# Keys of two more units transposed by TensorE, and unit inputs loaded one iteration later

## The chip, the core and the metric

The kernel runs on one core of one Trainium2 chip, as one program. The metric is the device time of a run in microseconds (us). Five engines take part, each with its own in-order instruction stream: TensorE (PE, with its weight loads as PEld), VectorE (DVE), ScalarE (ACT), GpSimd (POOL) and SyncE (SP). SP issues nearly all DMA transfers; POOL issues those that scatter rows.

## What is computed

A linear attention over 4 batches, 8 heads, 768 positions and head size 48, and then a mixture of 8 experts, one chosen for each of the 3072 tokens:

```python
for t in range(S):                                   # attention, B=4, H=8, S=768, D=48
    kt, vt, rt = (k[:, :, t], v[:, :, t], r[:, :, t])
    cur = np.einsum('bhd,bhe->bhde', u[None] * kt, vt)
    y[:, :, t] = np.einsum('bhd,bhde->bhe', rt, state + cur)
    state = w[None, :, :, None] * state + np.einsum('bhd,bhe->bhde', kt, vt)

logits = x @ w_gate + modality_bias[modality_id]     # x: y as 3072 tokens x 384
e_idx = np.argmax(logits, axis=1)                    # gate_w: the softmax at e_idx
for e in range(8):
    mask = e_idx == e
    out[mask] = gate_w[mask, None] * (np.maximum(x[mask] @ w1[e], 0.0) @ w2[e])
```

## The kernel before

The attention is cut into 24 units, one for each batch and chunk of 128 positions; units 0 to 3 are chunk 0 of the four batches, and so on. The main loop (L1195) goes over iterations `i` = 0 to 22 and works on several units at once, each a stage apart. The order of the instructions of every engine is the order in which this loop writes them (a manual schedule), so an instruction that waits holds up everything behind it on its engine. SP too is such a queue.

Each unit has two inputs. `turned(i)` (L322) loads `ud`: receptances and keys, already transposed in memory, 96 partitions x 2 x 512 f32, into one of four buffers. For the units in `TURNED` (1 to 12) it loads the receptances alone, half as much. `lines(i)` (L331) loads `kv`: keys and values with one token on each partition, 128 x 2 x 384 f32, into one of five buffers. For a unit in `TURNED`, `keys_turned` (L341) has PE transpose the keys of `kv` into PSUM (`pkT`, four transposes), and `keys` (L379) multiplies that instead of the loaded half of `ud`.

In iteration `i` the stages that matter here are, in the order in which they are written: PE transposes the rows of unit i-2 (`raised`, `pxT`, units 7 to 11), then the keys of unit i+2 (`keys_turned`), and then computes the scores of unit i+1 (`scores`, `psc`, from `rc` and `kc`). DVE copies the bonus `d` of unit i. Once that `d` is there, SP issues `turned(i + 5)`: the call `pace` (L350) makes SP load one value of `d` so that the issue falls at this time. POOL computes `rc` of unit i+3 from `ud` (`decay`) and `kt` of unit i+2 from `kv` (`carry`); DVE computes `kc` of unit i+2 (`keys`) and then the factor `sx` of unit i-1 (`factor`). Once that is there, SP issues `lines(i + 4)`. Then come the mask products `at` of unit i+1 on DVE and the values `py` and the state of unit i on PE (`values`, `py`, `pst`, ending with the bonus of unit i+1 at L393).

From iteration 8 on the weights of the first expert are loaded too, in six pieces of 128 x 1024 f32 (`raw`, L905, 0.5 MB each). The expert's number is computed from the first four units at the end of iteration 8 (`order`), and SP reads it (`ctl`, L1128). Pieces 0, 1 and 2 follow at once, pieces 3, 4 and 5 at the ends of iterations 9, 10 and 11 (L1152 and the lines behind it). ScalarE takes norms of the pieces (L908), PE sums them (L923, in iterations 11 and 13), and ScalarE and DVE split the pieces into two f16 parts `whi` and `wlo` in iterations 11 to 13. From iteration 13 on PE runs pieces of the first expert's two products beside the units.

Of the kernel before, what the change touches and what calls it, by code (L numbers as in the profile page):

```python
# [44 lines left out]
DENSE = 6  # L45
FADED = range(4, 14)
SHARED = range(9, 14)
TURNED = range(1, 13)
RAISED = range(7, 12)

NE = 9
# [13 lines left out]
class _Kernel:  # L65
# [256 lines left out]
    def turned(self, i):  # L322
# [3 lines left out]
        ud = self.ud[i % len(self.ud)]  # L326
        m = n if i in TURNED else 2 * n
        self.nc.sync.dma_start(ud[LOW:TOP, :m], self.pd[b * NCH + c].rearrange("j d n -> (j d) n")[:, :m])
# [12 lines left out]
    def keys_turned(self, i):  # L341

        if i in TURNED:
            u = self.ctx_[i]
# [751 lines left out]
    def run(self):  # L1096
        nc, tc, m = self.nc, self.tc, self.m
        units = self.units = [(b, c) for c in range(NCH) for b in range(B)]
        NU = len(units)
# [35 lines left out]
        def chain(*gs):  # L1135
            for g in gs:
                yield from g
# [39 lines left out]
        def route(i, d, f, *args):  # L1177
            for lo, hi in GROUPS:
                if hi - 1 + d == i and lo in groups:
                    f(groups[lo], *args)  # L1180

        def each(i, *fs):
            for f in fs:
                if live(i):
                    f(i)


        def fill(n=1):
            while n and fills:
                g = fills.pop(0)  # L1190
                if next(g, fills) is not fills:
                    fills.append(g)
                    n -= 1

        for i in range(NU - 1):  # L1195
            if i == 0:
                each(i + 5, self.turned)
                each(i + 4, self.lines)
            each(i - 2, self.raised)
            each(i + 2, self.keys_turned)  # L1200
            each(i + 1, self.scores)
            if i + 1 > EARLY:
                each(i + 1, self.own_keys)
            route(i, 3, lambda u: fills.append(self.choose(u)))
            route(i, 5, lambda u: fills.append(chain(self.place(u), self.ahead(ahead[u["lo"]], u)) if u["lo"] in ahead else self.place(u)))
            up, down = ups.get(i), ups.get(i - 1)
            if up is not None:
                self.s_up(up, 0)
            if down is not None:
                self.s_high(down, 1)  # L1210
                self.s_down(down, 0)
            self.token(i - 1) if i else None
            if ups.get(i - 2) is not None:
                self.s_take(ups[i - 2])
            if i and i - 1 == self.grp["lo"]:
                groups[i - 1] = self.grp
            fill()
            each(i, self.taken) if i else None
            each(i - 1, self.settled_state)
            if i - 2 in RAISED:  # L1220
                self.flipped(i - 2)
            if 0 < i < NU - 5:
                self.pace(self.ctx_[i]["d"])
                each(i + 5, self.turned)
            for j in range(2):
                each(i - 1, lambda i: self.state(i, j))
                fill()
            if down is not None:
                self.s_low(down, 1)
                self.s_due(down)  # L1230
            begin.get(i, lambda: None)()
            late = i >= NU - 3
            for k in range(1 if late else 2):
                for d in (6, 7):
                    route(i, d, self.send, 1)
                if k == 0:
                    each(i + 3, self.decay)
            if ups.get(i - 2) is not None:
                self.s_give(ups[i - 2])
            each(i + 2, self.carry)  # L1240
            route(i, 4, self.sign)
            each(i + 2, self.keys)
            if i + 2 <= EARLY:
                self.own_turned(i + 2)
            if i:
                fac = self.factor(i - 1)
                for _ in fac:
                    fill()
                if i < NU - 4:
                    self.pace(self.ctx_[i - 1]["g"]["sx"][:, self.ctx_[i - 1]["at_g"] :])  # L1250
                    each(i + 4, self.lines)
            self.own(i, 0)
            each(i - 1, self.high)
            mid.get(i, lambda: None)()
            for j in range(2):
                each(i + 1, lambda i: self.causal(i, j))
                fill()
            self.own(i, 1)
            if late:
                for d in (6, 7):  # L1260
                    route(i, d, lambda u: (self.rest(self.ctx_[i]["dv"][:1, DM - 1 :]), self.send(u, 1)))
            each(i - 1, self.low)
            if up is not None:
                self.s_high(up, 0)
                self.s_low(up, 0)
            fill()
            each(i - 1, self.flip)
            fill()
            self.values(i)
            if up is not None:  # L1270
                self.s_up(up, 1)
            if down is not None:
                self.s_down(down, 1)
            for p in range(2):
                for h in range(2):
                    c, r = divmod(i + 1 - 2 * p - h, B)
                    if r == 0 and 0 < c < NCH - 1:
                        self.fade(c, slice(2 * p, 2 * p + 2), range(2 * h, 2 * h + 2))
            if any(hi - 1 + d == i for lo, hi in GROUPS for d in (4, 5)):
                fill(99)  # L1280
            route(i, 2, self.logits)
            route(i, 4, self.count)
            for f in at.get(i, ()):
                f()
            for k in turns.get(i, ()):
                self.s_turn(k)
# [4 lines left out]
        i, j = NU - 2, NU - 1  # L1291
# [207 lines left out]
```

## Time and profile before

| | us |
|---|---|
| median of three runs | 348.51 (348.34 to 350.56) |
| the profiled execution | 350.38 |
| its span, first to last instruction | 348.6 |
| PE busy in the span | 327.6 (94%) |
| VectorE busy | 216.7 (62%) |
| ScalarE busy | 179.4 (51%) |
| GpSimd busy | 157.1 (45%) |

The profile is one execution; times in it count from the first instruction of the span. A busy PE isn't PE at its peak: matmuls are pipelined and their ends are modelled. "Idle before" names how long an engine did nothing ahead of an instruction, and what ended that. "Issue" stands there when the profile shows nothing that the engine waited for. The granted clock is given as a share of full speed, where 1.00 is 2.4 GHz and 0.50 is 1.2 GHz. The main loop takes the first 165 us or so; after it come the remaining routing and the experts.

### The profile page before, as it was taken

What the parts mean: (1) busy time and instruction counts of PE and PEld (TensorE: products, weight loads), DVE (VectorE), ACT (ScalarE), POOL (GpSimd) and SP (SyncE); (2) the same over time, 40 slices, a digit from 0 to 9 for tenths busy, and PEclk for the clock granted to TensorE, in tenths of its full rate; (3) what the DMA queues carried; (4) which work ended last, traced back from release to release, by engine and by line L of the source; (5) the groups of instructions that cost most, each with busy time, mean ns of one, the idle gap of its engine ahead of it and who ended that gap; (6) DMA issues with size and microseconds to landing.
All of it is one profiled execution on the core that took longest, in us unless ns stands there. A gap on an engine that the chain in (4) does not pass through costs nothing. (4 is left out here: it accounts for less than half of the span.)

```text
span 348.6 us, 15394 instructions
## 1 busy us (share of the span) xinstructions
PE 327.6 (94%) x5555; PEld 268.1 (77%) x5555; DVE 216.7 (62%) x740; ACT 179.4 (51%) x476; POOL 157.1 (45%) x230
## 2 busy tenths in 40 slices
PE   7998999697999999999998999999999999999993
PEld 3787998596878888887886777776888887777771
DVE  8878889489897977684668633349333332233951
ACT  7776885956965658465531222256222224552921
POOL 8987788756746865342167411113111210121221
PEclk9999999969999999999999999999999999999998
DMA  6766798997569999693235531127731121112120
GB/s 198 218 161 162 153 183 279 307 254 155 140 127 222 230 242 267 110 183 87 71 115 171 189 100 45 45 53 219 210 67 46 45 54 37 45 45 68 23 58 4
DMA packets 56797, 46.95 MB, mean 135 GB/s; under 512 B 42920, under 2 KB 50359, under 8 KB 56496
## 3 DMA queue, kind: packets, MB, share of 16 engines
q1 hardware_dynamic: 53552, 36.86, 44.7%
q0 software_dynamic: 3200, 9.47, 8.2%
q8 instruction: 31, 0.51, 0.7%
q14 instruction: 14, 0.11, 0.1%
HBM read 26.03 MB, written 11.83 MB: 109 GB/s over the span
## 5 line engine op out<-in xcount | busy, mean ns | idle before, releaser
L998 PEld LDWEIGHTS <-whi 128*128 128x128 f16 x1248 | 72.4, 98 | 4.0 <-issue 1.0
L1007 DVE SCALAR_TENSOR_TENSOR hl<-phb,hh 128x256 f16<-128x256 f32 (+1 forms) x48 | 24.5, 511 | 68.6 <-ACTq L1430 38.9
L1061 PEld LDWEIGHTS <-hh 128*128 128x128 f16 x416 | 39.1, 98 | 29.6 <-ACT hh L1002 1.7
L998 PE MATMUL phb<-mxT,whi 128*128 128x128 f16 x768 | 51.0, 219 | 0.0
L410 ACT ACTIVATE dv<-kv,d 128x48 f32<-128x48 f32 x172 | 43.1, 324 | 3.4 <-issue 2.2
L1002 ACT ACTIVATE hh<-phb 128x256 f16<-128x256 f32 (+1 forms) x48 | 21.4, 454 | 41.1 <-PE phb L998 18.7
L998 PEld LDWEIGHTS <-wlo 128*128 128x128 f16 x624 | 37.7, 98 | 1.0 <-DVE wlo L944 1.0
L371 POOL TENSOR_TENSOR rk<-rc,kc 112x512 f32<-112x512 f32 x20 | 25.8, 1288 | 27.0 <-DVE ebx L309 10.7
L430 DVE TENSOR_TENSOR at<-psc,mask 128x512 f32<-128x512 f32 x48 | 31.6, 681 | 3.6 <-PE psc L424 3.6
L967 POOL TENSOR_TENSOR seenb<-otb,putb 128x1 int32<-128x1 int32 x16 | 4.5, 283 | 64.2 <-ACTq L1430 50.9
L424 PE MATMUL psc<-rc,kc 64*64 64x128 f32 (+1 forms) x768 | 28.8, 280 | 4.7 <-issue 3.1
L359 POOL TENSOR_TENSOR rc<-ud,powr 112x512 f32<-112x512 f32 (+1 forms) x25 | 30.8, 1237 | 3.6 <-PE pst L393 2.2
L1061 PEld LDWEIGHTS <-hl 128*128 128x128 f16 x208 | 19.4, 98 | 15.1 <-issue 2.5
L424 PEld LDWEIGHTS psc<-rc,kc 64*64 64x64 f32 (+1 forms) x768 | 21.8, 134 | 10.7 <-issue 5.4
L666 POOL DMA_INDIRECT rows<-row,posi x24 | 25.0, 1041 | 11.2 <-DVE pr L743 3.8
L1061 PE MATMUL po<-whi,hh 128*128 128x384 f16 x136 | 27.7, 326 | 2.2 <-ACT whi L939 1.2
L998 PE MATMUL phb<-mxT,wlo 128*128 128x128 f16 x384 | 29.3, 219 | 0.0
L1061 PE MATMUL po<-whi,hl 128*128 128x384 f16 x136 | 28.0, 326 | 1.2 <-PEq L1495 0.7
L1061 PE MATMUL po<-wlo,hh 128*128 128x384 f16 x136 | 27.7, 326 | 0.0
L461 PE MATMUL py<-kv,at 128*64 128x48 f32 x768 | 27.2, 225 | 0.0
L998 PE MATMUL phs<-mxT,whi 128*128 128x128 f16 x432 | 27.2, 219 | 0.0
L944 DVE SCALAR_TENSOR_TENSOR wlo<-raw,ws,whi 128x1024 f16<-128x1024 f32 (+1 forms) x20 | 25.9, 1322 | 1.9 <-ACT whi L939 1.2
(272 smaller groups left out, 621.0 us busy)
## 6 DMA issues: line engine op xcount, KB each, us to landing
kv<-in_pt SPq DMA_DIRECT2D x21, 384.0 KB
raw<-in_w SPq DMA_DIRECT2D x12, 512.0 KB
ud<-in_pd SPq DMA_DIRECT2D x12, 384.0 KB
raw<-in_w SPq DMA_DIRECT2D x2, 1536.0 KB, 6.8
ud<-in_pd SPq DMA_DIRECT2D x12, 192.0 KB
rows<-pad SPq DMA_DIRECT2D x10, 193.0 KB
kv<-in_pt SPq DMA_DIRECT2D x6, 192.0 KB
rows<-row,posi POOLq DMA_INDIRECT x24, 5.9
```

What stands on the lines that cost most here:

```text
L359: nc.gpsimd.tensor_mul(u["rc"][:TOP, s], u["rT"][:TOP, s], self.powr[:TOP, s])
L371: nc.gpsimd.tensor_mul(u["rk"][:TOP], u["rc"][:TOP], u["kc"][:TOP])
L410: nc.scalar.activation(u["dv"][:, sl], u["v"][:, sl], AF.Copy, scale=u["d"][:, h : h + 1])
L424: nc.tensor.matmul(u["ps"][j][s, pr * P : (pr + 1) * P], u["kc"][r, pr, s], u["rc"][r, pr, :], start=True, stop=True)
L430: nc.vector.tensor_mul(u["at"][:, j * NPR : (j + 1) * NPR, :], u["ps"][j].rearrange("p (q t) -> p q t", q=NPR), self.mask.unsqueeze(1).to_ ...
L461: nc.tensor.matmul(py[t, sl], u["at"][:, j * NPR + pr, t], u["v"][:, sl], start=c == h == 0, stop=h == H - 1, skip_group_check=True)
L666: i = nc.gpsimd.indirect_dma_start(out=self.rows, out_offset=bass.IndirectOffsetOnAxis(ap=u["posi"][:, b : b + 1], axis=0), in_=u["row"][: ...
L944: self.nc.vector.scalar_tensor_tensor(self.wlo[:, sl], self.raw[:, sl], sc, self.whi[:, sl], ALU.mult, ALU.subtract)
L998: self.nc.tensor.matmul(ph[:, q * P : (q + 1) * P], w[:, c0 : c0 + P], self.xT[:, xq, t * P : (t + 1) * P], start=i == q == 0, stop=i == l ...
L1002: self.nc.scalar.activation(self.hh[:, f0 : f0 + fb, t * P : (t + 1) * P], p3, AF.Relu)
L1007: self.nc.vector.scalar_tensor_tensor(self.hl[:, f0 : f0 + fb, r], p3, 0.0, self.hh[:, f0 : f0 + fb, r], ALU.max, ALU.subtract)
L1061: self.nc.tensor.matmul(po[:, :DM], h[:, f, t * P : (t + 1) * P], w[:, c0 : c0 + DM], start=first, stop=last)
```

## The change

`TURNED` grows by units 13 and 14: PE transposes their keys as well, four transposes each, and their `ud` loads shrink to half. In iteration 8 no unit input is loaded. From iteration 9 on `turned` is called for unit i+4 in place of i+5 and `lines` for unit i+3 in place of i+4, so that each load from unit 13's `ud` and unit 12's `kv` on is issued one iteration later than before, and the last ones in iterations 19 and 20.

```diff
--- before.py
+++ after.py
@@ -45,7 +45,8 @@
 DENSE = 6
 FADED = range(4, 14)
 SHARED = range(9, 14)
-TURNED = range(1, 13)
+HELD = 8
+TURNED = range(1, 15)
 RAISED = range(7, 12)
 
 NE = 9
@@ -1219,9 +1220,10 @@
             each(i - 1, self.settled_state)
             if i - 2 in RAISED:
                 self.flipped(i - 2)
-            if 0 < i < NU - 5:
+            n = 5 - (i > HELD)
+            if 0 < i < NU - n and i != HELD:
                 self.pace(self.ctx_[i]["d"])
-                each(i + 5, self.turned)
+                each(i + n, self.turned)
             for j in range(2):
                 each(i - 1, lambda i: self.state(i, j))
                 fill()
@@ -1246,9 +1248,9 @@
                 fac = self.factor(i - 1)
                 for _ in fac:
                     fill()
-                if i < NU - 4:
+                if i < NU - n + 1 and i != HELD:
                     self.pace(self.ctx_[i - 1]["g"]["sx"][:, self.ctx_[i - 1]["at_g"] :])
-                    each(i + 4, self.lines)
+                    each(i + n - 1, self.lines)
             self.own(i, 0)
             each(i - 1, self.high)
             mid.get(i, lambda: None)()
```

SP's queue around the end of iteration 8, before. `ud1` and `kv2` are the buffers of unit 13's `ud` and unit 12's `kv`; `ud2` is that of unit 14:

```order
L550 DMA_TRANSPOSE xT4_840<-row4_839 128x6x128
L328 DMA ud1_86<-in_pd 96x1024
L338 DMA kv2_91<-in_pt 128x2x384
L1128 TENSOR_LOAD ctl_370
L1128 ISA x2
L905 ISA
L905 DMA raw_275<-in_w12 128x1024
L905 ISA
L905 DMA raw_275<-in_w12 128x1024
L905 ISA
L905 DMA raw_275<-in_w12 128x1024
L328 DMA ud2_87<-in_pd 96x1024
```

The same place after the change (lines are one further down):

```order
L551 DMA_TRANSPOSE xT4_840<-row4_839 128x6x128
L1129 TENSOR_LOAD ctl_370
L1129 ISA x2
L906 ISA
L906 DMA raw_275<-in_w12 128x1024
L906 ISA
L906 DMA raw_275<-in_w12 128x1024
L906 ISA
L906 DMA raw_275<-in_w12 128x1024
L329 DMA ud1_86<-in_pd 96x512
L339 DMA kv2_91<-in_pt 128x2x384
L906 ISA
```

The two loads, which stood ahead of the read of `ctl` and so of the weights, now stand behind three pieces of weights, and the `ud` load is half as large.

PE at the start of iteration 12, before: the rows of unit 10 are transposed (`pxT10`), and the scores of unit 13 follow:

```order
L543 LDWEIGHTS row8_1396
L543 MATMUL pxT10_1821<-id16_157,row8_1396 128x128
L424 MATMUL psc13_0_1828<-rc13_1578,kc13_1718 64x128
L424 MATMUL psc13_1_1829<-rc13_1578,kc13_1718 64x128
L424 MATMUL psc13_0_1828<-rc13_1578,kc13_1718 64x128
```

The same place after the change:

```order
L544 LDWEIGHTS row8_1388
L544 MATMUL pxT10_1818<-id16_157,row8_1388 128x128
L348 MATMUL pkT14_1825<-id32_148,kv4_93 112x128 x4
L425 MATMUL psc13_0_1830<-rc13_1570,kc13_1715 64x128
L425 MATMUL psc13_1_1831<-rc13_1570,kc13_1715 64x128
L425 MATMUL psc13_0_1830<-rc13_1570,kc13_1715 64x128
```

Four transposes of unit 14's keys from its `kv` buffer stand between them; in iteration 11 the same is so for unit 13. PE's transposes for unit 12 in iteration 10 are where they were. Nothing else moves on PE; on VectorE two `kc` products read `pkT` instead of `ud`.

## Rows read from the trace of the kernel before

**Rows 1.** The page: engines (part 1), and the clock in 40 slices (part 2).

```profile
PE 327.6 (94%) x5555; PEld 268.1 (77%) x5555; DVE 216.7 (62%) x740; ACT 179.4 (51%) x476; POOL 157.1 (45%) x230
...
PEclk9999999969999999999999999999999999999998
```

**Rows 2.** PE in order of time: start us, us, line, operation, [idle before, releaser].

```profile
59.77 0.34 PE L543 MATMUL pxT<-id,row 128*128 128x128 f16 x3 [0.31 <-DVE off L760]
59.95 0.60 PE L347 MATMUL pkT<-id,kv 128*112 128x128 f32 x4
60.48 0.87 PE L424 MATMUL psc<-rc,kc 64*64 64x128 f32 x20
63.01 0.65 PE L424 MATMUL psc<-rc,kc 64*64 64x128 f32 x12 [1.66 <-issue]
63.60 0.88 PE L454 MATMUL py<-st,rc 112*64 112x96 f32 x16
...
66.69 0.51 PE L543 MATMUL pxT<-id,row 128*128 128x128 f16 x6
67.12 0.66 PE L424 MATMUL psc<-rc,kc 64*64 64x128 f32 x14
69.20 1.53 PE L424 MATMUL psc<-rc,kc 48*64 48x128 f32 x18 [1.42 <-issue]
70.67 0.19 PE L923 MATMUL py<-wssq,onesb 128*128 128x3 bf16 x1
...
76.95 1.10 PE L424 MATMUL psc<-rc,kc 64*64 64x128 f32 x32
```

**Rows 3.** Stretches: busy us of PE, PEld, DVE, ACT, POOL; clock, DMA share, GB/s.

```profile
55.50:58.00 2.50, 2.50 (x85) 2.50 (x81) 2.50 (x13) 2.32 (x7) 2.10 (x3) 1.00 0.77 178
58.00:60.00 2.00, 1.69 (x47) 1.46 (x45) 1.56 (x6) 1.07 (x4) 1.81 (x3) 1.00 0.97 346
60.00:64.50 4.50, 2.84 (x63) 2.25 (x62) 2.76 (x14) 4.44 (x13) 4.30 (x5) 1.00 1.01 308
...
69.00:76.00 7.00, 6.80 (x112) 6.45 (x113) 5.04 (x17) 3.14 (x7) 4.61 (x6) 0.51 0.92 271
...
84.00:88.00 4.00, 1.54 (x25) 1.16 (x24) 3.19 (x5) 0.91 (x5) 0.85 (x2) 1.00 0.25 53
...
98.00:156.00 58.00, 57.91 (x1223) 49.34 (x1221) 46.19 (x165) 38.65 (x124) 32.34 (x38) 1.00 0.93 201
...
98.50:101.00 2.50, 2.50 (x80) 2.42 (x77) 2.50 (x12) 2.24 (x9) 0.86 (x1) 1.00 0.59 157
240.00:244.00 4.00, 3.77 (x23) 1.92 (x22) 3.93 (x13) 1.29 (x3) 1.46 (x1) 1.00 1.03 363
63.00:69.15 6.15, 4.77 (x128) 4.23 (x127) 3.46 (x13) 6.08 (x18) 3.80 (x4) 1.00 1.05 315
```

**Rows 4.** The page, part 3: the queue named instruction: packets, MB, share.

```profile
q8 instruction: 31, 0.51, 0.7%
```

**Rows 5.** SP's queue in order of time: start us, us, what it issued.

```profile
51.05 0.38 SPq L338 DMA_DIRECT2D kv<-in_pt  x1
55.45 1.45 SPq L905 DMA_DIRECT2D raw<-in_w  x3
57.08 0.51 SPq L328 DMA_DIRECT2D ud<-in_pd  x1
57.77 0.51 SPq L338 DMA_DIRECT2D kv<-in_pt  x1
...
72.55 0.38 SPq L338 DMA_DIRECT2D kv<-in_pt  x1
...
98.26 0.34 SPq L328 DMA_DIRECT2D ud<-in_pd  x1
```

**Rows 6.** ScalarE in order of time: the first norm of the weights.

```profile
60.02 1.06 ACT L908 ACTIVATE junk<-raw 128x1024 f16<-128x1024 f32 x1 [0.95 <-DMA raw<-in_w]
```

**Rows 7.** GpSimd in order of time: the decayed receptances of unit 18.

```profile
101.37 1.28 POOL L359 TENSOR_TENSOR rc<-ud,powr 112x512 f32<-112x512 f32 x1
```

## The prediction

> **What bounds the kernel now.** I read the page first: TensorE (PE) is busy 94% of the span, and its clock row shows two slices below 9 in the body, the first of them slice 9, at 70 to 78 us [rows 1]. So I went to PE's timeline there, iterations 10 to 12 of the main loop. The reader is to see two idle times in the middle of a run of score matmuls (`psc`, L424): 1.66 us before 63.01 and 1.42 us before 69.20, both put to "issue", that is to nothing the profile shows [rows 2]. Only the first matmuls of such a run carry waits, so it isn't data. Then I read stretches: DMA is full from 58 us on (share 0.97 and more), and from 69 to 76 us the granted clock is 0.51, the 1.2 GHz level, though PE is busy; before and after it is 1.00, the 2.4 GHz level [rows 3]. Between the start of the work at 63 us and the second gap lie 128 matmuls and 127 weight loads [rows 3]; the queue named "instruction" moved 31 packets of 0.51 MB in all, 16.5 kB each [rows 4]. I read both gaps as PE waiting for its next block of instructions behind full DMA queues. That is an inference from spacing and load. From 98 to 156 us PE is busy 57.91 of 58 us [rows 3]: what is late before that is late at the end.
>
> The Trainium skill, page "Runtime: NRT & Kernel Launch", section "Instruction fetch mechanics", says that instructions come by DMA in blocks of 256, the next fetched while the present one runs, and calls the cost mostly hidden. The trace agrees with the 256 and not with "hidden": 1.66 and 1.42 us.
>
> **The change, part by part.** Times of the sum are those of the profiled execution: 350.38 us, a span of 348.6 and 1.8 around it. The median of the three runs is 348.51, 1.9 below; I add the sum to the median.
>
> (a) *Unit 12's keys and values arrive later.* Before, its `kv` load was issued at 51.05, 8.9 us ahead of the transposes that read it (`pkT`, 59.95, start of iteration 10) [rows 2, 5]. After the change it is issued where unit 13's is now, at 57.77, and unit 13's `ud` where unit 14's is now, at 57.08 [rows 5]. Both stand behind the three `raw` loads of 55.45 in SP's queue, and the order shows nothing that lets them past. If the queue is worked off in order, the bytes up to and with `kv` of unit 12 are 3 x 524 + 197 + 393 = 2163 kB (from the shapes). The stretches give 178 GB/s x 2.5 us = 445 kB by 58 us and 346 x 2 = 692 more by 60, 1137 together; the other 1026 kB at 308 GB/s take 3.3 us: 63.3 [rows 3]. From last byte to release I take raw's own row: its first 524 kB are through at 58 + 79/346 = 58.2 by the same count, and ScalarE, which waited for them, starts at 60.02 [rows 6]: 1.8 us. So `kv` is there at 65.1. Bounds: at 363 GB/s from 58 us (the fastest stretch) and with no release time 62.7; at 271 GB/s from 60 us 65.6 [rows 3]. From the start of `pkT` to the 20th `psc` matmul PE took 61.35 - 59.95 = 1.40 us, so the place that was reached at 63.01 is reached at 65.1 + 1.4 = 66.5 [rows 2]: **+3.5 us** (bounds +1.1 and +4.0). I take the middle estimate since it uses the stretch itself. The first instruction gap lies inside this wait and no longer counts.
>
> On this the Trainium skill, page "DMA: Bandwidth & Descriptors", section "Queues, rings and completion order", says that each DMA engine takes one queue's descriptors in ring order, while completion need not follow that order. No run here yet shows it for `kv`. By ring order the sum is as above; if a later load could finish early, the first rival below holds.
>
> Behind `pkT` on PE everything of iteration 10 queues up; on VectorE the key product `kc`, the factor `sx` of unit 9 and the mask product wait behind it. The `sx` also paces SP's next `kv` issue, so the loads of units 13 on slip as well; those DMA queues are then empty, which is (b).
>
> (b) *The second gap goes.* Its block of instructions would now be fetched during and after the wait, with 3.8 MB in place of 4.2 MB queued up to the fifth `raw` load, and part of that issued later. I take **-1.4 us** (bounds -1.4 and 0).
>
> (c) *Eight transposes more.* Four took 60.48 - 59.95 = 0.53 us of PE, start to start [rows 2]; two units: **+1.1 us** (bounds 0.5, if they fall into waits, and 1.1). VectorE's `kc` reads PSUM instead of SBUF for these two units, with the same shape; no cost. The two halved `ud` loads save 197 kB or 0.6 us of DMA at 346 GB/s for each, inside (a) and (b).
>
> (d) *Unit 14's keys are late too.* Its `kv` is issued in iteration 11, in the place of 72.55, which is 1.88 us after the small matmul L923 at 70.67 [rows 2, 5]; VectorE does L923's scales ahead of the pacing factor. A lone load of this size, issued at 98.26, had moved its 157 x 2.5 = 393 kB by 101.0, 2.7 us later [rows 3, 5]. So it is there 4.6 us after L923, or 6.4 with the release time of (a). PE arrives at `pkT` of unit 14 after 0.12 + 3.09 + 0.43 = 3.6 us at full clock (the values 63.60 to 66.69, then the turn of the rows until 67.12), or 6.3 at half clock [rows 2]. The wait is 1.0 to 2.8 us, or 0 to 0.1. I take **+1.6**, nearer the lower half of the first, as small matmuls of the count also stand there.
>
> (e) *The clock.* Before, it was low for 7 us after two gaps that sum to 3.1 us, which costs about 7 x 0.49 = 3.4 us [rows 3]. After, PE stands from 60.1 to 65.1, 5 us in one piece. I expect one such fall again, at another place: **0** (bounds -3.4, none, and +3.4, a second one at (d)).
>
> (f) *Loads with one iteration less of lead, iterations 12 to 20.* They cost nothing on PE: `rc` of unit 18 on GpSimd starts at 101.37, 3.1 us after the issue that would now be its own (98.26), so GpSimd may wait up to 1.4 us there [rows 5, 7]. Behind it on GpSimd queue `kt` and the row sends; `rc` is read by PE an iteration or more later. The cover is GpSimd's free time: 45% busy [rows 1]. If it were gone, each of some six iterations would give up to 1.4 us. Two late pairs of loads on SP (units 23 and 22) stand ahead of the transposing stores, which wait for the same factor anyway.
>
> Sum: 3.5 - 1.4 + 1.1 + 1.6 + 0 = **+4.8 us**, 348.5 + 4.8 = 353.3 us.
>
> **Rivals.** *Unit 12's load is hidden* (not slower). If later loads share the DMA engines with `raw`, `kv` could be there by 61.6, and then PE reaches 63.01 as before. That is the point from which it decides. For it: both gaps then shrink to at most the first, and the clock may stay up. Against it: the first 524 kB of `raw` themselves took until 60.02 [rows 6], and even issued alone at 57.77 with the 2.7 us of a lone load `kv` is there at 60.5 at the earliest. It would give -1.4 - 3.4 + 1.1 + 0.8 (half of (d)) = -2.9: 345.6 us.
>
> *The clock doesn't fall, or is back before PE has its data.* For it: at 84 to 88 us PE was busy only 1.54 of 4 us and the clock stayed at 1.00 [rows 3]. Against: two shorter gaps brought it down at 69 us. Sum 4.8 - 3.4 = +1.4: 349.9 us.
>
> *It falls twice*, the second time at unit 14's wait: 4.8 + 3.4 = +8.2: 356.7 us.
>
> *Absorbed.* The 2.5 us in which PE stands at 84 to 88 us could take up part of the delay [rows 3]. Against it: that wait is for VectorE and ScalarE, whose work there follows PE's scores of unit 13 and so slips with them. With 2.5 us taken up: +2.3, 350.8 us.
>
> **How the numbers follow.** Forecast 0.47 (its own range 350.5 to 356); hidden load 0.15; clock saved 0.15; second fall 0.13; absorbed 0.10. One per cent, 3.5 us, is about what a measurement of this kernel can tell from no change: below 345.0 is faster, above 352.0 slower. Slower: 0.36 of the forecast's 0.47, all of the second fall and a little of "absorbed", 0.51. Faster: a third of the hidden load, 0.05. The rest, 0.44, lies within 1%. The range from 346 to 357 leaves out half of the hidden load, half of the second fall and the forecast's tails, less than 0.2.
>
> **What would show it.** Right: in PE's timeline of the changed kernel `pkT` of unit 12 starts some 5 us after the transposes of unit 8's rows, released by a DMA of `kv`; no issue gap follows in `psc` of unit 12; `pkT` of unit 14 waits again for 1 to 3 us; the granted clock is low for about 7 us once; from iteration 14 on every start is 4 to 5 us later, to the end. Wrong: `pkT` of unit 12 starts before 61.6 (then (a) falls, and the queue isn't worked off in order); the gaps stay (then they aren't instruction blocks kept back by DMA); or the starts agree again from 98 us on (absorbed).

## The result, and the profile after

The changed kernel took 353.31 us (median of six runs, 351.86 to 355.69), the kernel before 349.22 beside it on the same chip: a ratio of 1.0124, with a 95% interval from 1.0086 to 1.0163. Measured again on another chip it was 353.72 against 349.65, 1.0115 (1.0064 to 1.0167). So the change costs about 4.1 us. The profiled execution of the changed kernel took 352.36 us, with a span of 350.6.

The page of the changed kernel, engines (part 1) and the clock in 40 slices (part 2):

```profile
PE 328.5 (94%) x5563; PEld 269.0 (77%) x5563; DVE 212.0 (60%) x740; ACT 179.2 (51%) x476; POOL 155.8 (44%) x230
...
PEclk9999998598999999999999999999999999999999
```

Beside [rows 1] there are eight matmuls more, and the slow slices are 7, 8 and 10 (8, 5 and 8 tenths; a slice is 8.8 us) in place of 9. PE's timeline shows why. Its columns are those of [rows 2]; lines are one further down than before.

```profile
53.00 1.10 PE L425 MATMUL psc<-rc,kc 64*64 64x128 f32 x32
...
58.60 0.34 PE L544 MATMUL pxT<-id,row 128*128 128x128 f16 x3 [0.31 <-DVE off L761]
64.55 1.10 PE L348 MATMUL pkT<-id,kv 128*112 128x128 f32 x4 [5.61 <-DMA kv<-in_pt]
65.58 1.99 PE L425 MATMUL psc<-rc,kc 64*64 64x128 f32 x32
71.63 0.51 PE L544 MATMUL pxT<-id,row 128*128 128x128 f16 x6
71.97 0.60 PE L348 MATMUL pkT<-id,kv 128*112 128x128 f32 x4
72.50 1.10 PE L425 MATMUL psc<-rc,kc 64*64 64x128 f32 x32
73.54 0.18 PE L924 MATMUL py<-wssq,onesb 128*128 128x3 bf16 x1
77.36 0.24 PE L621 MATMUL pr<-oh,warm 128*128 128x8 f16 x4 [0.56 <-DVE row L612]
77.64 0.49 PE L544 MATMUL pxT<-id,row 128*128 128x128 f16 x6
78.83 0.62 PE L348 MATMUL pkT<-id,kv 128*112 128x128 f32 x4 [0.70 <-DMA kv<-in_pt]
79.38 1.47 PE L425 MATMUL psc<-rc,kc 64*64 64x128 f32 x32
85.52 1.28 PE L425 MATMUL psc<-rc,kc 64*64 64x128 f32 x32
89.60 0.17 PE L924 MATMUL py<-wssq,onesb 128*128 128x3 bf16 x1 [0.69 <-ACT row L498]
95.49 1.10 PE L425 MATMUL psc<-rc,kc 64*64 64x128 f32 x32
```

The transposes of unit 12's keys (64.55) wait 5.61 us for their `kv`. The score matmuls of units 11 (65.58) and 12 (72.50) then run in one piece: both issue gaps of [rows 2] are gone. Unit 13's transposes (71.97) don't wait, unit 14's (78.83) wait 0.70 us.

To compare places one thing has to be taken out. The scores of unit 10, which the change doesn't touch, start at 53.00 here and at 54.13 in the kernel before; this execution was 1.13 us ahead by then. The same place in the kernel before, the scores of unit 15, and two waits that will matter, from its PE timeline:

```profile
54.13 1.10 PE L424 MATMUL psc<-rc,kc 64*64 64x128 f32 x32
...
85.49 0.68 PE L998 MATMUL phs<-mxT,wlo 128*128 128x128 f16 x9 [0.86 <-DVE wlo L944]
87.77 0.17 PE L923 MATMUL py<-wssq,onesb 128*128 128x3 bf16 x1 [1.60 <-ACT row L497]
...
93.65 1.10 PE L424 MATMUL psc<-rc,kc 64*64 64x128 f32 x32
```

With 1.13 us added to the times after the change, the scores of unit 11 start 6.2 us later than before (60.48 to 66.71), those of unit 12 6.5 (67.12 to 73.63), of unit 13 3.6 (76.95 to 80.51), and of unit 15 3.0 (93.65 to 96.62). The span's end is 3.1 later; the two profiled executions themselves are 2.0 us apart, so they show less than the 4.1 of the medians. What is lost at unit 12's keys is partly given back twice: once in iterations 11 and 12, where before had its second gap and its slow clock, and once between 84 and 90 us, where before waited 0.86 and 1.60 us and the changed kernel only 0.69.

The second profile of the changed kernel, from the other chip, needs no such shift: its scores of unit 10 start at 54.04. The scores of units 10 and 15 in its PE timeline:

```profile
54.04 1.10 PE L425 MATMUL psc<-rc,kc 64*64 64x128 f32 x32
...
96.51 1.10 PE L425 MATMUL psc<-rc,kc 64*64 64x128 f32 x32
```

There unit 12's transposes start at 66.23, 6.3 us later than before, the scores of unit 13 4.1 later (at 81.06) and those of unit 15 2.9 later. The clock falls only once, from 61.4 to 71.6 us.

Stretches of the changed kernel (columns as in [rows 3]): the two with the clock at 0.50, then the settled loop, then the whole disturbed part, 55 to 108 us:

```profile
59.30:69.40 10.10, 4.85 (x64) 4.18 (x66) 3.19 (x16) 6.47 (x16) 5.22 (x6) 0.51 0.79 258
80.00:83.40 3.40, 3.40 (x62) 3.07 (x54) 2.91 (x12) 3.36 (x10) 2.58 (x4) 0.50 0.77 187
...
98.00:156.00 58.00, 57.22 (x1175) 47.98 (x1172) 45.69 (x163) 36.88 (x121) 32.34 (x36) 1.00 0.95 210
55.00:108.00 53.00, 44.48 (x983) 39.25 (x980) 40.49 (x134) 37.81 (x98) 32.18 (x33) 0.87 0.68 186
```

and the last of these for the kernel before:

```profile
55.00:108.00 53.00, 46.32 (x1065) 40.99 (x1055) 44.10 (x140) 40.05 (x104) 35.48 (x37) 0.94 0.80 204
```

From such rows each kernel's loss can be added up: what PE stood still in these 53 us, and half of what it was busy at the lower clock. Before: 53 - 46.32 = 6.7 still, and 6.80 x 0.49 = 3.3 by the clock (the stretch 69 to 76 us in [rows 3]), 10.0 in all. After: 8.5 still, 4.85 x 0.49 + 3.40 x 0.50 = 4.1 by the clock, and 1.1 for the eight transposes, 13.7. The second profile of the changed kernel gives 13.6 (9.9 still, 5.37 x 0.49 = 2.6 by the clock, 1.1). The difference, 3.7 us, lies between the 3.0 by which unit 15 lags in the same two executions and the 4.1 of the medians, so the sum is good to some 0.7 us. It is used once more below.

SP's queue (SP's start us, us for the issue) and two waits of GpSimd, changed kernel:

```profile
54.29 3.20 SPq L906 DMA_DIRECT2D raw<-in_w  x3
57.62 0.35 SPq L329 DMA_DIRECT2D ud<-in_pd  x1
58.15 0.41 SPq L339 DMA_DIRECT2D kv<-in_pt  x1
...
75.42 0.38 SPq L339 DMA_DIRECT2D kv<-in_pt  x1
```

```profile
63.44 1.25 POOL L360 TENSOR_TENSOR rc<-ud,powr 112x512 f32<-112x512 f32 x1 [5.17 <-DMA ud<-in_pd]
...
136.64 1.71 POOL L360 TENSOR_TENSOR rc<-ud,powr 112x512 f32<-112x512 f32 x1 [2.86 <-DMA ud<-in_pd]
```

The reader sees unit 12's `kv` issued at 58.15, 3.9 us behind the first of three weight pieces (compare [rows 5]), and at hand 6.4 us later. Unit 13's `ud`, just ahead of it, keeps GpSimd waiting for 5.17 us.

### The profile page after: what moved, and what is told of

It is laid out like the page before. It is cut to its first block, busy times and chain, and to the rows that moved or that the text cites. A ratio compares the mean times of both kernels' runs of the same rounds, so it can differ in the third digit from the quotient of the medians.

```text
span 350.6 us, 15408 instructions
## 1 busy us (share of the span) xinstructions
PE 328.5 (94%) x5563; PEld 269.0 (77%) x5563; DVE 212.0 (60%) x740; ACT 179.2 (51%) x476; POOL 155.8 (44%) x230
## 5 line engine op out<-in xcount | busy, mean ns | idle before, releaser
L360 POOL TENSOR_TENSOR rc<-ud,powr 112x512 f32<-112x512 f32 (+1 forms) x25 | 31.6, 1266 | 13.8 <-DMA ud<-in_pd 13.1
L667 POOL DMA_INDIRECT rows<-row,posi x24 | 25.5, 1064 | 10.8 <-issue 3.7
L425 PE MATMUL psc<-rc,kc 48*64 48x128 f32 (+1 forms) x768 | 28.2, 285 | 0.8 <-POOL rc L360 0.8
L425 PEld LDWEIGHTS psc<-rc,kc 48*64 48x64 f32 (+1 forms) x768 | 21.8, 137 | 6.4 <-issue 2.2
L462 PEld LDWEIGHTS py<-kv,at 128*64 128x64 f32 x768 | 26.1, 143 | 0.7 <-issue 0.7
```

Source lines behind the costliest of these rows:

```text
L360: nc.gpsimd.tensor_mul(u["rc"][:TOP, s], u["rT"][:TOP, s], self.powr[:TOP, s])
L425: nc.tensor.matmul(u["ps"][j][s, pr * P : (pr + 1) * P], u["kc"][r, pr, s], u["rc"][r, pr, :], start=True, stop=True)
L462: nc.tensor.matmul(py[t, sl], u["at"][:, j * NPR + pr, t], u["v"][:, sl], start=c == h == 0, stop=h == H - 1, skip_group_check=True)
L667: i = nc.gpsimd.indirect_dma_start(out=self.rows, out_offset=bass.IndirectOffsetOnAxis(ap=u["posi"][:, b : b + 1], axis=0), in_=u["row"][: ...
```

## The experiments

All ratios are against the kernel before on the same chip. The chips differ in level (its medians were 344.97, 349.65, 344.85 and 347.06 us in the four groups), so only ratios are compared between groups.

### Unit 12's `kv` early, all else changed

```diff
-                if i < NU - n + 1 and i != HELD:
+                if i < NU - n + 1 and i != HELD + 1:
```

> The changed kernel, but unit 12's kv is loaded in iteration 8 again, ahead of the weights; everything else as changed. If the late kv of unit 12 makes the loss: the wait of 5.6 us in front of pkT of unit 12 is gone, and the time falls from 353.3 to 349 to 351 us (what stays is 1.1 us for the transposes and up to 1.6 for unit 14). If the eight transposes or the late ud loads make it: 352.5 to 354 us, with no wait at pkT of unit 12 and the lateness at another place.

1.0017 (0.9978 to 1.0056). Nearly all of the loss is gone. PE's timeline, the transposes of units 12, 13 and 14:

```profile
58.60 0.60 PE L348 MATMUL pkT<-id,kv 128*112 128x128 f32 x4
...
67.32 1.10 PE L348 MATMUL pkT<-id,kv 128*112 128x128 f32 x4 [2.83 <-DMA kv<-in_pt]
...
75.77 0.62 PE L348 MATMUL pkT<-id,kv 128*112 128x128 f32 x4 [0.33 <-DMA kv<-in_pt]
```

Unit 12's don't wait any more. What no theory foresaw: now unit 13's wait 2.83 us, since they came early enough to meet their own `kv`, which is still behind the weights. The loss of one late load, 1.0124 and 1.0115 less 1.0017, is 0.98 to 1.07%, some 3.6 us, with some 2 us either way by the intervals.

### The transposes alone

```diff
-TURNED = range(1, 13)
+TURNED = range(1, 15)
```

(in the kernel before)

> The kernel before, with the keys of units 13 and 14 transposed by TensorE and all loads issued where they were. If the late kv makes the loss: 349 to 350.5 us, that is at most the 1.1 us of the transposes more than before, or slightly less if 394 kB less of ud shorten the two idle times in psc. If the transposes make it: 352.5 to 354 us.

1.0038 (0.9991 to 1.0085): +1.3 us, with an interval from -0.3 to +2.9. PE's timeline, the transposes of units 12 and 13:

```profile
58.61 0.60 PE L347 MATMUL pkT<-id,kv 128*112 128x128 f32 x4
...
67.99 1.10 PE L347 MATMUL pkT<-id,kv 128*112 128x128 f32 x4 [4.04 <-DMA kv<-in_pt]
```

Again unit 13's keys wait, for a `kv` that was issued at 57.77, right behind the weights as in the kernel before [rows 5]. Turning the keys puts PE's transposes in front of that load. There is no issue gap in the scores of units 11 and 12 here. The wait can't be what replaces the first gap, since the scores of unit 11 run from 59.14, ahead of it; what differs there is told under the blocks of instructions below.

### The later loads alone

```diff
-TURNED = range(1, 15)
+TURNED = range(1, 13)
```

(in the changed kernel)

> The changed kernel's load order with the keys of units 13 and 14 loaded, not transposed. If the late kv of unit 12 makes the loss: pkT of unit 12 waits some 5 to 6 us as in the changed kernel; unit 14's wait and 1.1 us of transposes are gone; 351 to 352.5 us. If the transposes make it: 349.2 us, no change against before. If the late ud makes it: 353 us or more, since ud is twice as large for units 13 and 14.

1.0249 (1.0147 to 1.0352) from four runs: far more than the first two theories said. The third, late `ud`, allowed such a time, but the next section shows late `ud` loads alone to cost nothing. A second measurement:

> The changed kernel with the keys of units 13 and 14 not turned (their ud loads in full, no transposes for them), a second time. Its first figure, 1.0249 of the time before from four runs, lies 4.3 us above that of the changed kernel (1.0124), though it has 1.1 us less work on TensorE. Theory (the 197 kB more of unit 13's ud, which stand ahead of unit 12's kv, and the 197 kB of unit 14's cost far more than the 0.6 us each of the prediction): 1.020 to 1.030, and unit 12's kv again lands 12.5 us or more after the issue of the first weight piece. Rival (scatter of the landing, which was 12.2 us in another kernel with half the load ahead): 1.008 to 1.016, landing 10.3 to 11.5 us.

1.016 (1.0103 to 1.0218). Unit 12's transposes in PE's timeline, first run and second:

```profile
68.31 1.10 PE L348 MATMUL pkT<-id,kv 128*112 128x128 f32 x4 [8.69 <-DMA kv<-in_pt]
```

```profile
65.77 1.10 PE L348 MATMUL pkT<-id,kv 128*112 128x128 f32 x4 [5.73 <-DMA kv<-in_pt]
```

The first weight piece was issued at 54.97 and 55.39, so `kv` was at hand 13.3 and 10.4 us after it, by the same program. Most of the first figure may be scatter of that landing; that is not shown. The later loads alone account for the whole loss. Both figures lie above both of the changed kernel, though the intervals overlap, so whether turning the keys of units 13 and 14 costs its 1.1 us, or saves something by the halved `ud` ahead of `kv`, stays open.

### Late `ud`, `kv` as early as before

```diff
-                if i < NU - n + 1 and i != HELD:
+                if i < NU - 4:
                     self.pace(self.ctx_[i - 1]["g"]["sx"][:, self.ctx_[i - 1]["at_g"] :])
-                    each(i + n - 1, self.lines)
+                    each(i + 4, self.lines)
```

> The changed kernel, but all kv loads are issued in the iterations of before; only the ud loads come an iteration later, and units 13 and 14 are transposed. If the late kv makes the loss: GpSimd still waits about 5 us for unit 13's ud, which nobody on PE feels, and the time is 348 to 350.5 us. If the late ud makes it: 352.5 to 354 us.

1.0032 (0.9986 to 1.0078), no more than the transposes alone (1.0038). Late `ud` loads cost nothing that can be measured, though GpSimd waits for them. The first run of this section kept unit 12's `kv` alone early and comes out the same, so the later `kv` of units 13 on cost nothing that can be measured either.

### Two weight pieces moved behind unit 12's `kv`

```diff
-            plan(O + max(q - 2, 0), first(q))
+            plan(O + max(q - 2, 1 if q else 0), first(q))
```

> The changed kernel, with pieces 1 and 2 of the weights issued after unit 12's kv (in iteration 9) in place of ahead of it. If the queue is worked off in order, 1048 kB less stand ahead of kv: it lands some 3.4 us sooner after the first piece's issue, about 6 to 7 us after it instead of 10, pkT of unit 12 waits 1.5 to 3 us, and the ratio to before falls to 1.000 to 1.006. If all loads under way share the engines, so that the order within the queue does not matter: the landing, the wait of 5 to 6 us and the ratio of 1.012 stay.

1.0049 (1.0005 to 1.0094), beside 1.0115 for the changed kernel on the same chip:

> The changed kernel once more, beside the kernel before on this chip: a ratio of 1.009 to 1.016, that is some 3 to 5.5 us more, with a wait of 5 to 6 us for unit 12's kv. If the first measurement was a matter of the chip or of the clock's phase: a ratio of 1.00.

SP's queue and PE's wait with the two pieces behind, then PE's wait in the changed kernel run beside it:

```profile
54.58 0.38 SPq L906 DMA_DIRECT2D raw<-in_w  x1
55.41 0.33 SPq L329 DMA_DIRECT2D ud<-in_pd  x1
56.38 1.08 SPq L339 DMA_DIRECT2D kv<-in_pt  x1
57.68 1.43 SPq L906 DMA_DIRECT2D raw<-in_w  x3
```

```profile
62.57 1.10 PE L348 MATMUL pkT<-id,kv 128*112 128x128 f32 x4 [3.34 <-DMA kv<-in_pt]
```

```profile
66.23 1.10 PE L348 MATMUL pkT<-id,kv 128*112 128x128 f32 x4 [6.19 <-DMA kv<-in_pt]
```

With 1048 kB less ahead of it `kv` is at hand 8.0 us after the first piece's issue instead of 10.8 (10.3 in the first profile), and PE waits 3.34 us instead of 6.19. The ratio fell as the order of the queue has it, but the landing came 1 us later than the 6 to 7 us expected. The trace shows more. Each of these loads has sixteen completion updates, as many as there are DMA engines (read here as one for each engine's share), and PE starts within 0.06 us of the last. The eighth update comes 6.0 us after the first piece's issue here and 9.4 us after it in both profiles of the changed kernel: 3.4 us sooner, the figure that was expected for 1048 kB. The last one trails the eighth by 2.0 us here, by 0.9 and 1.4 there. So what stands ahead in SP's queue does hold `kv` back.

### Less behind unit 12's `kv`

```diff
-            plan(O + max(q - 2, 0), first(q))
+            plan(O + max(q - 2, 0) + (q == 3), first(q))
```

> The changed kernel with the fourth weight piece (0.5 MB), which is issued 0.6 us behind unit 12's kv, put off by one iteration; what stands ahead of kv is unchanged. Theory that the queue is worked off in order: kv of unit 12 lands as in the changed kernel, 10.0 to 10.8 us after the issue of the first piece, and the wait of unit 12's transposes stays 5 to 6.2 us. Rival (what is issued behind shares the DMA engines with kv): it lands 1 to 1.5 us sooner, 8.7 to 9.3 us after the first piece's issue, with a wait of 4 to 4.7 us.

One run, 350.9 us. PE's wait, and a stretch of that wait:

```profile
66.67 1.10 PE L348 MATMUL pkT<-id,kv 128*112 128x128 f32 x4 [7.58 <-DMA kv<-in_pt]
```

```profile
65.00:66.60 1.60, 0.00 (x0) 0.00 (x0) 0.00 (x0) 0.00 (x0) 1.44 (x2) 0.50 0.14 52
```

That is 12.2 us after the first piece's issue (54.44): neither theory's number. The completion updates show where the scatter lies. Unit 13's `kv` in the kernel with the transposes alone and in the one with late `ud` has the same 2163 kB up to and with it, so there are five loads to compare, and three with more or less:

| kernel, load | kB up to and with it | first update | eighth | last, us after the first piece's issue |
|---|---|---|---|---|
| changed, two profiles, unit 12 | 2163 | 8.8, 8.6 | 9.4, 9.4 | 10.2, 10.8 |
| less behind, unit 12 | 2163 | 9.5 | 10.2 | 12.2 |
| late `ud`, unit 13 | 2163 | 9.4 | 10.2 | 11.8 |
| transposes alone, unit 13 | 2163 | 9.8 | 10.7 | 13.8 |
| later loads alone, two profiles, unit 12 | 2360 | 10.5, 9.3 | 11.2, 9.8 | 13.3, 10.3 |
| two pieces behind, unit 12 | 1114 | 5.4 | 6.0 | 8.0 |

With 2163 kB the eighth update lies within 1.3 us and the last within 3.6: it is the last few shares of a load that come at such different times. In the stretch above PE waits for `kv` while the sixteen DMA engines are busy to 0.14 in the mean. By the eighth update the half megabyte that follows `kv` doesn't delay it (10.2 us without it, 9.4 with it). Why some engines trail stays open.

### Are the issue gaps blocks of instructions?

```diff
+        for q in range(8 if i == 9 else 0):
+            nc.tensor.matmul(u["ps"][q % 2][:, :64], self.ones16, self.warm[:, :64], start=True, stop=True)
```

(eight weight loads and eight matmuls more ahead of the scores of unit 9, in the kernel before)

> The kernel before with eight weight loads and eight matmuls of 64 columns more on PE, in front of the scores of unit 9 (their results are overwritten). If the idle times in psc of units 11 and 12 are waits for blocks of 256 instructions, each comes eight pairs earlier in the program: after 12 matmuls of psc of unit 11 in place of 20, and after 6 of unit 12 in place of 14. If they come from something that the matmul at that place needs: after 20 and after 14.

One run, 352.93 us. The scores of units 11 and 12 in PE's timeline:

```profile
60.99 0.65 PE L427 MATMUL psc<-rc,kc 64*64 64x128 f32 x12
63.43 1.55 PE L427 MATMUL psc<-rc,kc 64*64 64x128 f32 x20 [1.79 <-issue]
...
70.69 1.10 PE L427 MATMUL psc<-rc,kc 64*64 64x128 f32 x32
```

In [rows 2] the gap stood behind 20 of the 32 matmuls, here behind 12: it moved by just the eight that were put in. So it belongs to a place in the instruction stream, not to data or to a time. The second gap, expected behind 6 matmuls of unit 12, isn't there.

Two counts from the traces settle what these gaps are. One is the number of matmuls and weight loads that PE has done before a gap. The other is the end of the last packet of 16.4 kB on the queue named instruction [rows 4] ahead of the gap's end:

| PE instructions before the gap | packet | kernel: gap, us (from the packet's end to PE's next matmul, us) |
|---|---|---|
| 2497 | ninth | shifted 0.41 (1.32) |
| 2753 | tenth | before 1.66 (1.39); shifted 1.79 (1.29); turned with weights behind, two profiles (below), 0.88 (1.35), 0.53 (1.36) |
| 3009 | eleventh | before 1.42 (1.31); turned with weights behind 0.99 (1.40), 1.05 (1.30) |
| 3265 | twelfth | transposes alone 0.52 (1.40); turned with weights behind 0.67 (1.35), 0.92 (1.44) |
| 3521 | thirteenth | transposes alone 0.71 (1.58) |

The places are 256 instructions apart in five executions of four kernels, and each time PE goes on 1.3 to 1.6 us after a packet. So both gaps of [rows 2] are waits for blocks of 256 instructions, as the prediction inferred. (Three more issue gaps, of 0.20 to 0.32 us past 81 us, are at other places.) The second gap is missing here because its packet was through at 68.42, while PE, at the lower clock from 63.0 to 69.9 us, came to the scores of unit 12 at 70.69.

What makes a packet late is less clear. In the four executions with the gap at 2753 the tenth packet starts at 59.6 to 61.2 us; in the ten others it starts at 54.6 to 56.7, and PE finds its block there. The prediction's "behind full DMA queues" is not shown: the packets of [rows 2]'s gaps took 1.00 and 1.09 us once they had started, and the gap of 0.41 us here stood at a DMA share of 0.50 (54.4 to 56.8 us).

The Trainium skill, page "Runtime: NRT & Kernel Launch", section "Instruction fetch mechanics", calls the cost of such fetches mostly hidden. In ten of the fourteen profiles it is hidden at the tenth block; in four it cost 0.53 to 1.79 us.

### The order of the weights in the kernel before

With units 13 and 14 turned and the two weight pieces behind unit 13's loads (both diffs above, in the kernel before):

> The kernel before with the keys of units 13 and 14 transposed and pieces 1 and 2 of the weights issued after unit 13's kv. In order: the wait of 4.0 us that the transposes alone put in front of pkT of unit 13 is gone, so is a part of the two idle times in psc, and the time is 1 to 4 us below before. If the order within the queue does not matter: as with the transposes alone, 0 to 1.5 us above before.

0.9966 (0.9929 to 1.0004). No transposes wait, and the gaps are 0.88 and 0.99 us. A second measurement:

> The kernel before with units 13 and 14 turned as well, and with the weights' pieces 1 and 2 issued behind unit 13's ud and kv; loads as early as before. A second measurement of the kernel whose first gave 0.9966 of the time before (0.9929 to 1.0004). Theory (the kv loads of units 12 to 14 all come in time, the two instruction gaps of 1.66 and 1.42 us shrink to under 1 us each, and the fall of the clock is met once as before): 0.994 to 0.999. Rival (the first figure was chance, the order of the weights is worth nothing beside the 1.1 us of the transposes): 1.000 to 1.005.

1.0052 (1.0019 to 1.0085). Its gaps had shrunk, the first to under 1 us as expected:

```profile
61.97 0.65 PE L424 MATMUL psc<-rc,kc 64*64 64x128 f32 x12 [0.53 <-issue]
...
68.43 0.88 PE L424 MATMUL psc<-rc,kc 48*64 48x128 f32 x22 [1.05 <-issue]
```

The second gap now stands behind 10 matmuls of unit 12 in place of 14: the four transposes of unit 13 ahead of them moved it by four. Still there is no gain. The two intervals don't even meet, so two chips can differ by more than the intervals say, here by 0.9%; both figures lie within about half a per cent of the kernel before. The weights' order alone:

> The kernel before with nothing but the weights' pieces 1 and 2 issued one iteration's step later, behind unit 13's ud and kv. Theory that the gain of the kernel with both edits comes from the order of the weights: the gaps in the score matmuls of units 11 and 12 shrink from 1.66 and 1.42 us to under 1 us each, and without the eight transposes (1.1 us) it is 1 us faster than that one: 0.991 to 0.997. Rival (the halved ud loads of units 13 and 14, 0.4 MB less in the full queues, brought the gain): gaps of 1.3 us or more stay, 0.998 to 1.003.

1.0111 (1.0061 to 1.0161): slower, against both theories. There is no issue gap at all in its scores, and yet it loses. Three rows of PE's timeline and one stretch:

```profile
69.03 0.16 PE L923 MATMUL py<-wssq,onesb 128*128 128x3 bf16 x1 [1.66 <-ACT row L497]
...
84.71 0.68 PE L998 MATMUL phs<-mxT,wlo 128*128 128x128 f16 x9 [1.66 <-DVE wlo L944]
87.00 0.17 PE L923 MATMUL py<-wssq,onesb 128*128 128x3 bf16 x1 [1.60 <-ACT row L497]
```

```profile
65.90:72.40 6.50, 4.84 (x84) 4.45 (x79) 2.12 (x14) 4.22 (x14) 0.97 (x2) 0.50 1.03 251
86.50:96.30 9.80, 9.30 (x131) 9.20 (x131) 8.26 (x15) 7.42 (x16) 7.01 (x6) 0.50 0.52 142
55.00:108.00 53.00, 45.53 (x943) 40.35 (x938) 42.03 (x135) 38.33 (x100) 32.50 (x33) 0.84 0.78 200
```

The weights come later, so ScalarE's norms do, and PE waits for a ScalarE instruction behind them (`row`) where it had not: 1.66 us before 69.03, nothing at that place in [rows 2]. The clock falls twice: from 65.7 us on, ahead of that wait and after shorter ones (0.23, 0.64 and 0.31 us from 62.2 on), and again for some 10 us from 86.2 on, in the second of two waits of 1.66 and 1.60 us. The sum: 53 - 45.53 = 7.5 still, 4.84 x 0.50 + 9.30 x 0.50 = 7.1 by the clock, 14.6 against 10.0 before. Of the 4.6 us more, 3.8 are the clock. None of these kernels is clearly faster than the kernel before.

## Why the prediction was right, point by point

The forecast was 353.3 us by a mechanism that the runs confirm: unit 12's `kv` waits behind the weights. That the median hit it so closely is partly luck: the sum of +4.8 against +4.1 measured hides errors of both signs.

- **(a), the late `kv`: +3.5, measured +4.1.** The transposes started 10.3 us after the first piece's issue, where the working gives 65.1 - 55.45 = 9.7. Aligned, they start 65.68 - 59.95 = 5.7 us later than before, less the 1.66 of the first gap: 4.1, just above the upper bound of 4.0; in the second profile it is 4.7. The count by bytes left out other traffic: 3.1 MB moved from the first piece's issue to the landing (10.26 us at 303 GB/s) in place of 2163 kB. Its bounds were too narrow, since they allowed for the rate of the queue but not for the scatter of the last shares of a load (10.2 to 13.8 us). The mechanism is shown by taking it away (1.0017) and by halving what stands ahead (1.0049).
- **(b), the second gap: -1.4.** The scores of unit 12 run in one piece (72.50), and both gaps are waits for blocks of instructions, as inferred. But the reason given, that the block would be fetched during the wait, is shown only in part: ten of fourteen profiles, four of them without a wait ahead of unit 11's scores, have no gap there at all, so the kernel before may often run without these gaps, and then there is less to win.
- **(c), the transposes: +1.1.** The run with them alone gives +1.3 (-0.3 to +2.9), which bears the size but can't settle it, since unit 13's wait and the missing gaps are in it too. Whether the 0.6 us of DMA for each halved `ud` are a saving is not shown.
- **(d), unit 14's `kv`: +1.6, measured 0.70** (0.59 in the second profile, 0.33, 0.63 and 0.71 in three variants). Its issue stood 1.88 us behind the small matmul, to the hundredth as worked out (75.42 - 73.54), and it was at hand 5.3 us behind it, inside the 4.6 to 6.4. What was mis-sized is PE's way there: 78.13 - 73.54 = 4.6 us instead of 3.6. A wait of 0.56 us for VectorE (before 77.36) is part of it.
- **(e), the clock: 0.** The clock costs 4.1 us in place of 3.3, in falls of 10.1 and 3.4 us, so "falls twice" came true in form, but not at its price: the first one lay mostly over the wait itself, where PE had nothing to run slowly (4.85 us busy of 10.1). In the second profile it falls once, as forecast, and costs 2.6.
- **(f), less lead: 0.** Right for PE, as the run with late `ud` alone shows; its scores wait 0.8 us in all for `rc`, before and after. Wrong in its bound: GpSimd waited up to 2.86 us (at 136.64), not 1.4, in the settled part, at a DMA share of 0.95 (98 to 156 us), while the bound came from a load in a stretch with 0.59 [rows 3]. The cover held: PE is busy 57.22 of 58 us from 98 to 156 us.
- **The rival "absorbed" was partly real.** The argument against it, that the work of VectorE and ScalarE at 84 to 88 us slips with PE's scores, was wrong: 2.46 us of waits shrank to 0.69, so 1.8 us were taken up there. In the second profile one wait of 1.37 us is left, so 1.1 were taken up. With (d) too large by 0.9 the terms were thus 2.7 too high in the first profile, and with (a) 0.6 and the clock 0.8 too low. That leaves +3.5, near the 3.7 of the sum over the stretch.
- **"From iteration 14 on every start is 4 to 5 us later"** held only in part: 3.0 us aligned, 1.8 unaligned (93.65 to 95.49), since the profiled execution was ahead for reasons outside the change. In the second profile it is 2.9 with no shift.

One alternative that was not weighed at all is the one that two experiments ran into: with `kv` of unit 12 early, PE meets unit 13's `kv` behind the same weights (2.83 and 4.04 us). In the changed kernel this is hidden, since the first wait comes ahead of it.

## What to carry to other kernels

A small load that is put one step later is not one step late: look at what it then stands behind in its queue, and count bytes from the first issue of that burst to the reader. Give the landing a range from several loads, not from one, since its last shares scatter most. When two waits stand at the same time (an instruction block, a late load, another engine's result), taking one away shows the next, so the gain has to be worked out with all of them on the page.

## What the runs showed of the hardware that was not expected

- A load's landing behind full queues scatters by 3 us or more at the same bytes ahead (10.2 to 13.8 us with 2163 kB; 10.3 and 13.3 us with 2360), and most of that lies between its eighth completion update and its last. The Trainium skill, page "DMA: Bandwidth & Descriptors", section "Two DMAs through the same engine are not ordered", says that nothing orders transfers across the 16 engines. The trace agrees: the sixteen updates of one `kv` are 1.0 to 4.0 us apart from first to last, and in the kernel with less behind the first update of unit 14's `ud`, issued behind unit 12's `kv`, comes at 64.66, 2.0 us ahead of the last of that `kv` (66.63).
- Where PE crosses into the next 256 of its instructions it can stand for up to 1.79 us, always at the same counts (2753, 3009, 3265) whatever the kernel, and goes on 1.3 to 1.6 us after a packet of 16.4 kB.
- Executions differ by some 1.2 us at 38 us, before any of the edits act: the scores of unit 7 start at 37.8 to 38.2 us in seven profiles, at 39.0 to 39.5 in six and at 38.6 in one. All four with the gap in unit 11's scores are among the six, but two of the six (the second profiles of the changed kernel and of the later loads alone) have no such gap. Why is open.
- The clock is lost in places, not in proportion to idle time: waits of 0.86 and 1.60 us at 84 to 88 us left it at 1.00 [rows 3], and with waits of 1.66 and 1.60 us at the same place the clock was at 0.50 for 9.8 us, which cost 4.7 us, more than the waits themselves. In the shifted kernel, too, waits of 1.67 and 1.60 us (before 86.40 and 88.68) came ahead of 6.9 us at 0.51 (90.3 to 97.2).
